# A first MLP on token tiles of 384, 384, 512, 512, 512 instead of six of 384, with single buffers for keys, queries and values

## The chip, the cores and the metric

The kernel runs on one core of one Trainium2 chip, as one program. The metric is the device time of an execution in microseconds (us). The kernel before takes 785.8 us, the median of three runs (784.78 to 785.98).

## The reference, cut to what matters

Three stages, all in fp32, over 4 batches x 576 positions = 2304 tokens of width 512 (8 heads x 64).

```
scores = q @ k.T / sqrt(64)                       # per batch and head, 576 x 576
masks  = plain window of 32 keys      (heads 0-3)
         32 keys at a stride of 4     (heads 4-7, "dilated")
x  = softmax(where(mask, scores, -1e9)) @ v       # laid out as tokens x 512
x  = max(x @ w1, x @ w2, x @ w3) @ w_out          # first MLP, 512 -> 768 -> 512
h  = x @ w_in                                     # second MLP, 512 -> 2048 -> 512
g  = (a0 + a1*h + a2*h^2 + a3*h^3) / (1 + |b0|*|h| + |b1|*h^2 + 1e-6)
out = g @ w_out
```

## The kernel before, in words

**Arithmetic.** Both MLPs keep the precision of fp32 with split operands: an operand is held as a high part (`x1h`, `hh`, `x2h`, `gh`) and a low part (`x1l`, `hl`, `x2l`, `gl`), and each product is three matmuls (`mm3`, L535 to L540): high x high, high x low, low x high. ScalarE (ACT) makes the high part with a copy, VectorE (DVE) the low part with a subtraction. The first MLP's weights come as 8-byte words and are converted on the chip in five steps named `L`, `up`, `bits`, `hi`, `lo`; the 32 tiles of the second MLP's weights are converted one per "tick" during the first MLP, put back to HBM as `w2d`, and fetched again as `w2s` by `load_w2` (L598), each fetch with a copy on ACT and a subtraction on DVE.

**Attention.** The tokens go through attention in 12 chunks of 192, three per batch. A chunk has a plain half (`p`) and a dilated half (`d`), and each runs `S` (scores on TensorE, PE), `MX` (mask add and row maximum, DVE), `D` (subtract, DVE), `E` (exp, ACT), `SM` and `SB` (sum and normalisation, DVE), `X` (transposes on PE in two groups) with `XC` (copies on ACT), `V` (times the values, PE), and `VH`, `VL` (the split of the result into `x1h` and `x1l`).

**First MLP.** It runs in six units of 384 tokens (`TU`). A unit has 18 groups of 12 matmuls (6 blocks of the inner width x 3 weight matrices; each group is followed by a copy or a maximum out of PSUM) and 4 groups of 18 for its output (`Y`), so 288 matmuls in 22 slots. The output goes to HBM as `x2d`.

**Second MLP.** Tiles of 512, 512, 512, 384, 384 tokens, 16 slices each: 12 matmuls make `h`, ACT and DVE evaluate the fraction, and 12 (or 9) matmuls add it into `acc`. A slice's `acc` matmuls stand three slices behind its `h` matmuls.

**Order of the work.** The table `START` writes out chunks 0 to 3 and unit 0 word by word; `W:n` puts 4n small matmuls on a zero tile in front (`keep_warm`, L177). From unit 1 on, unit u's groups are emitted one per slot, and beside each stands one row of the table `UNIT` for chunks 2(u+1) and 2(u+1)+1: two chunks during each of units 1 to 4, none during unit 5. Every engine runs its instructions in the order in which a scheduler then put them; the `order` rows below show that order. TensorE's weight loads run beside its matmuls.

**Buffers and queues.** Queries have two buffers per half (`QA`), keys two, values one; loads of the first chunks go on the SP queue, those of the later ones on POOL's, where the writes of `w2d` and `x2d` stand too. Of the 32 tiles of `w2s`, 7 (`W2A`) are fetched as the last unit starts, 18 as that unit gives up the first MLP's weights, and 7 after it (`w2c`, L746).

## Time and profile before

| | |
|---|---|
| median of 3 runs | 785.8 us |
| the profiled execution's own time | 785.84 us |
| its span, first to last instruction | 784.1 us |
| PE busy | 778.1 us, 99% |
| DVE busy | 589.5 us, 75% |
| ACT busy | 466.2 us, 59% |
| granted TensorE clock | 1.000 |

PE counts as busy while a matmul is in flight, and matmuls overlap, so a busy PE is read by the distance between the starts of neighbouring matmuls. "Idle before" names what ended an engine's wait. Times are us from the span's start, unless marked ns.

### The profile page before, as it was taken

The page shows a single profiled execution, that of the slowest core. Times are in us where ns is not written, and L with a number is a line of the kernel's source. Part 1 is how long each engine was busy: PE and PEld are TensorE (multiplying, and loading weights), DVE is VectorE, ACT ScalarE, POOL GpSimd, SP SyncE. Part 2 cuts the span into 40 slices and gives each one's busy share as a digit, 9 for nine tenths or more (in the row PEclk, how much of TensorE's full clock was granted, in tenths as well). Part 3 has the DMA queues.
Part 4 walks back from the last instruction along what each step waited for, and adds up shares of the span by engine and source line. Part 5 has one row for each costly group of instructions (what it writes and reads, how often), then busy time and mean ns, then how long its engine had stood idle before and what let it go on. Part 6 is the DMA issues. An engine that isn't in the chain of part 4 may idle for free.

```text
span 784.1 us, 12858 instructions
## 1 busy us (share of the span) xinstructions
PE 778.1 (99%) x4964; PEld 712.4 (91%) x4964; DVE 589.5 (75%) x1066; ACT 466.2 (59%) x907; POOL 55.8 (7%) x106
## 2 busy tenths in 40 slices
PE   9999999999999999999999999999999999999998
PEld 8999999999999999999988888888888889989996
DVE  5999366456465475367299999888988889888885
ACT  5898242332333333265397778766877678777774
POOL 0000221201211201100100001000010001000000
PEclk9999999999999999999999999999999999999999
DMA  9993346745655544184500011000110011000001
GB/s 335 405 407 122 127 154 217 247 134 189 214 173 189 174 144 161 44 292 123 173 0 1 1 54 54 1 1 0 41 55 0 1 41 54 1 1 22 21 0 41
DMA packets 28606, 86.52 MB, mean 110 GB/s; under 512 B 3664, under 2 KB 5328, under 8 KB 28544
## 3 DMA queue, kind: packets, MB, share of 16 engines
q1 hardware_dynamic: 20208, 55.41, 20.3%
q0 software_dynamic: 8336, 30.28, 11.0%
q8 instruction: 39, 0.64, 0.3%
q14 instruction: 23, 0.19, 0.1%
HBM read 67.85 MB, written 17.83 MB: 109 GB/s over the span
## 4 chain that ended last, share of the span: by engine, by line
PE 85%; issue 10%; DVE 2%; DMA 1%; POOL 1%; ACT 0%; POOLq 0%; SPq 0%; ACTq 0%; DVEq 0%
PE mm L538 9%; PE mm L539 9%; PE mm L540 9%; PE acc L826 8%; PE acc L825 8%; PE acc L827 8%; PE h L539 8%; PE h L540 8%; PE h L538 8%; PE sc L295 3%; PE tpp L374 2%; PE pv L405 1%; PE pv L397 1%; PE sc L179 1%; DMA raw<-in_w_in_dram 1%
## 5 line engine op out<-in xcount | busy, mean ns | idle before, releaser
L538 PE MATMUL mm<-x1h,w1s 128*128 128x384 f32 x432 | 146.8, 340 | 0.0
L539 PE MATMUL mm<-x1l,w1s 128*128 128x384 f32 x432 | 144.8, 335 | 0.0
L540 PE MATMUL mm<-x1h,w1s 128*128 128x384 f32 x432 | 144.5, 335 | 0.0
L540 PE MATMUL h<-x2h,w2s 128*128 128x512 f32 (+1 forms) x320 | 117.7, 368 | 0.0
L538 PE MATMUL h<-x2h,w2s 128*128 128x512 f32 (+1 forms) x320 | 117.6, 368 | 0.0
L539 PE MATMUL h<-x2l,w2s 128*128 128x512 f32 (+1 forms) x320 | 117.6, 367 | 0.0
L825 PE MATMUL acc<-w2s,gh 128*128 128x512 f32 x288 | 112.2, 389 | 0.2 <-ACT gh L806 0.2
L826 PE MATMUL acc<-w2s,gh 128*128 128x512 f32 x288 | 112.3, 390 | 0.0
L827 PE MATMUL acc<-w2s,gl 128*128 128x512 f32 x288 | 109.3, 390 | 0.0
L781 DVE SCALAR_TENSOR_TENSOR q<-q,cs,ab 128x512 f32<-128x512 f32 (+1 forms) x80 | 55.7, 696 | 37.8 <-ACT ab L775 37.5
L538 PEld LDWEIGHTS mm<-x1h,w1s 128*128 128x128 f32 x432 | 81.0, 188 | 1.0
L539 PEld LDWEIGHTS mm<-x1l,w1s 128*128 128x128 f32 x432 | 81.2, 188 | 0.0
L540 PEld LDWEIGHTS mm<-x1h,w1s 128*128 128x128 f32 x432 | 81.1, 188 | 0.0
L774 ACT ACTIVATE q<-h 128x512 f32<-128x512 f32 (+1 forms) x80 | 43.9, 548 | 58.8 <-PE h L540 57.8
L559 DVE TENSOR_TENSOR m<-mm,m 128x384 f32<-128x384 f32 x72 | 39.7, 553 | 40.4 <-PE mm L540 40.3
L539 PEld LDWEIGHTS h<-x2l,w2s 128*128 128x128 f32 x320 | 60.1, 188 | 8.1
L538 PEld LDWEIGHTS h<-x2h,w2s 128*128 128x128 f32 x320 | 60.0, 188 | 8.1
L540 PEld LDWEIGHTS h<-x2h,w2s 128*128 128x128 f32 x320 | 60.1, 188 | 7.5
L806 ACT ACTIVATE gh<-p 128x512 fp32r<-128x512 f32 (+1 forms) x80 | 47.6, 595 | 31.1 <-DVE p L800 30.4
L825 PEld LDWEIGHTS acc<-w2s,gh 128*128 128x128 f32 x288 | 54.1, 188 | 11.6 <-ACT gh L806 0.7
L827 PEld LDWEIGHTS acc<-w2s,gl 128*128 128x128 f32 x288 | 54.0, 188 | 11.3
L826 PEld LDWEIGHTS acc<-w2s,gh 128*128 128x128 f32 x288 | 54.0, 188 | 10.9
...
## 6 DMA issues: line engine op xcount, KB each, us to landing
...
```

The costliest lines, as they stand in the source:

```text
L295: nc.tensor.matmul(o[h], lhsT=lq[:, h], rhs=rk, start=not pem, stop=not pem or n % G == G - 1)
L374: nc.tensor.transpose(tp[:, i, :], sv[:, G * j + i, :], ident[:Q, :Q])
L538: nc.tensor.matmul(o, lhsT=lh, rhs=rh, start=(i == 0), stop=False)
L539: nc.tensor.matmul(o, lhsT=lh, rhs=rl, start=False, stop=False)
L540: pe_at[0] = nc.tensor.matmul(o, lhsT=ll, rhs=rh, start=False, stop=(i == n - 1))
L559: nc.vector.tensor_tensor(out=m1[u, f], in0=o, in1=m1[u, f], op=ALU.max)
L774: nc.scalar.activation(out=s["q"], in_=s["h"], func=AF.Square)
L781: nc.vector.scalar_tensor_tensor(out=s["q"], in0=s["q"], scalar=cs[:, 5:6], in1=s["ab"], op0=ALU.mult, op1=ALU.add)
L806: nc.scalar.activation(out=s["gh"], in_=s["p"], func=AF.Copy)
L825: nc.tensor.matmul(o, lhsT=gh, rhs=w[:, 0:512], start=(c == 0), stop=False)
L826: nc.tensor.matmul(o, lhsT=gh, rhs=w[:, 512:1024], start=False, stop=False)
L827: nc.tensor.matmul(o, lhsT=gl, rhs=w[:, 0:512], start=False, stop=(c == F2 - 1))
```

## The change

The first MLP's units become 384, 384, 512, 512, 512 tokens (`SZ1`), so that there are five: 288 matmuls each, the last three on 512 columns. A chunk of 192 can now end in the middle of a unit, so `pieces` writes its split into one or two units. The eight chunks after `START` go three during unit 1, three during unit 2, two during unit 3 (`FIRST`, `UNITS`), none during unit 4. The 36 ticks of the weight conversion are spread over 66 slots, not 88.

Buffers: queries and keys have one each (the next chunk's queries are fetched when this chunk's scores are done, the next batch's keys after the batch's last scores), batch 0's keys lie in an `x1` buffer and chunk 1's values where `hh` and `hl` come later, and `w2s` has 3 tiles at the last unit's start, 18 during it and 11 after it. The plain queries of chunks 0 to 3 come without the zero blocks of their block-diagonal form (`qf`, half the bytes); their scores are 12 matmuls of half the rows and columns, not 6. `START` is written anew.

```
-mk qp0 mkB kp0 W:14 S0:p qd0 MX0:p kd0 kp1 E0:p W:7 S0:d,mm qp1 SM0:p SB0:p,act MX0:d D0:d W:1 S1:p
...
+mkB mk qp0 kp0 W:8 S0:p,pv MX0:p qd0 kd0 E0:p W:7 S0:d,mm L SM0:p SB0:p qd1 W:5 X0:p,1,pv MX0:d D0:d
+up X0:p,0,pv XC0:p,0 kp1 qp1 W:1 S1:d E0:d bits hi SM0:d MX1:d S1:p,mm lo L XC0:p,1 E1:d v0 v1 qd2
...
-UNIT = """
...
+UNITS = {3: """
 Sa:p
...
-    TU = 2 * CH
-    NU = NT // TU
+    SZ1 = [384, 384, 512, 512, 512]
+    NU = len(SZ1)
+    AT1 = [sum(SZ1[:u]) for u in range(NU)]
+    T1 = max(SZ1)
+    FIRST = {2: 4, 3: 7, 4: 10}
...
-    W2A = 7
+    W2A = 3
...
-    spare = []
+    keys0 = {}
+
+    def unit_x1(u):
+        if u not in x1:
+            x1[u] = [com.tile([128, NP * T1], F32R, tag=tag, bufs=2, name=f"{tag}{u}")
+                     [:, 0:NP * SZ1[u]].rearrange("p (c t) -> p c t", c=NP)
+                     for tag in ("x1h", "x1l")]
+        return x1[u]
...
         if b not in at_k:
-            at_k[b] = (
-                at.tile([128, S // 32, 2, 32], F32, tag="kTp", bufs=2, name=f"kTp{b}"),
-                at.tile([128, 8, S // 4], F32, tag="kTd", bufs=2, name=f"kTd{b}"),
-            )
+            if b == 0:
+                for tag in ("x1h", "x1l"):
+                    keys0[tag] = com.tile([128, NP * T1], F32, tag=tag, bufs=2, name="keys0")
+                kTp, kTd = [keys0[tag][:, 0:2 * S] for tag in ("x1h", "x1l")]
+            else:
+                kTp, kTd = [at.tile([128, 2 * S], F32, tag=tag, name=f"{tag}{b}")
+                            for tag in ("kTp", "kTd")]
+            at_k[b] = (kTp.rearrange("p (n a t) -> p n a t", a=2, t=32),
+                       kTd.rearrange("p (n m) -> p n m", n=8))
         kTp, kTd = at_k[b]
-        queue = nc.sync if b < 3 else nc.gpsimd
+        queue = nc.sync if b < 2 else nc.gpsimd
...
-        queue = nc.sync if c < 3 * QA else nc.gpsimd
-        if g == "p":
-            t = at.tile([128, 2 * BP, 2 * QP], F32, tag="qTp", bufs=QA, name=f"qTp{c}")
-            queue.dma_start(out=t.rearrange("p n w -> p (n w)"), in_=qp_in[c])
-        else:
-            t = at.tile([128, 8, 2 * M], F32, tag="qTd", bufs=QA, name=f"qTd{c}")
-            queue.dma_start(out=t.rearrange("p n w -> p (n w)"), in_=qd_in[c])
+        queue = nc.sync if c <= MASK_PE else nc.gpsimd
+        pool = cv_p[0] if c in (1, 3) else at
+        src = qd_in[c] if g == "d" else qf_in[c] if c < MASK_PE else qp_in[c - MASK_PE]
+        n = src.shape[1]
+        t = pool.tile([128, n if pool is not at else 2 * BP * 2 * QP], F32, tag="qT" + g,
+                      name=f"qT{g}{c}")[:, 0:n]
+        queue.dma_start(out=t, in_=src)
+        t = t.rearrange("p (n w) -> p n w", n=8 if g == "d" else 2 * BP)
         at_raw[c, g] = t
...
+        if c == 1:
+            vp, vd = [com.tile([128, 2 * T1], F32, tag=f"hhl{f}", name=f"v1_{f}") for f in (0, 1)]
...
-                for h in (slice(0, QP), slice(QP, Q)) if plain and not pem else (slice(0, Q),):
-                    nc.tensor.matmul(o[h], lhsT=lq[:, h], rhs=rk,
+                for h in (slice(0, QP), slice(QP, Q)) if plain else (slice(0, Q),):
+                    if plain and pem:
+                        l, r = lq[h], rk[h]
+                    else:
+                        l, r = lq[:, h], rk
+                    nc.tensor.matmul(o[h], lhsT=l, rhs=r,
                                      start=not pem, stop=not pem or n % G == G - 1)
-            if c >= 2 * QA:
-                load_q(c + QA, g)
-            if g == "d" and ci == 0 and 1 < b < B - 1:
+            if c >= MASK_PE:
+                load_q(c + 1, g)
+            if g == "d" and ci == NC - 1 and 0 < b < B - 1:
                 load_k(b + 1)
...
-        def split_of(g):
-            pv = grp["v" + g]
+        def pieces(g):
             at_p = slice(0, 2) if g == "p" else slice(2, 4)
-            return pv, x1h[:, at_p, tok], x1l[:, at_p, tok]
+            t0, t1 = CH * c, CH * c + CH
+            for u in range(NU):
+                a, z = max(t0, AT1[u]), min(t1, AT1[u] + SZ1[u])
+                if a < z:
+                    h, l = unit_x1(u)
+                    to = slice(a - AT1[u], z - AT1[u])
+                    yield grp["v" + g][:, :, a - t0:z - t0], h[:, at_p, to], l[:, at_p, to]
 
         def VH(g):
-            src, dh, _ = split_of(g)
-            nc.scalar.activation(out=dh, in_=src, func=AF.Copy)
+            for src, dh, _ in pieces(g):
+                nc.scalar.activation(out=dh, in_=src, func=AF.Copy)
 
         def VL(g):
-            src, dh, dl = split_of(g)
-            nc.vector.tensor_sub(dl, src, dh.bitcast(F32))
+            for src, dh, dl in pieces(g):
+                nc.vector.tensor_sub(dl, src, dh.bitcast(F32))
...
-        for row in UNIT.strip().split("\n"):
+        first, some = FIRST[u], FIRST.get(u + 1, NCH) - FIRST[u]
+        for row in UNITS[some].strip().split("\n"):
             for word in row.replace("-", "").split():
                 op, _, arg = word.partition(":")
-                c = 2 * u + "abc".index(op[-1])
+                c = first + "abcd".index(op[-1])
...
-    def m1_mm(u, f, j, cols=slice(0, TU)):
+    def m1_mm(u, f, j, cols=None):
         if (u, f, j) not in m1:
-            m1[u, f, j] = bank("mm", "mm")[:, 0:TU]
+            m1[u, f, j] = bank("mm", "mm")[:, 0:SZ1[u]]
+        cols = cols or slice(0, SZ1[u])
...
-        hh = com.tile([128, TU], F32R, tag=f"hh{f}", name=f"hh{f}")
-        nc.scalar.activation(out=hh, in_=m1[u, f], func=AF.Copy)
-        m1["h", u, f] = [hh, None]
+        hhl = com.tile([128, 2 * T1], F32R, tag=f"hhl{f}", name=f"hhl{f}")
+        n = SZ1[u]
+        m1["h", u, f] = [hhl[:, 0:n], hhl[:, T1:T1 + n]]
+        nc.scalar.activation(out=hhl[:, 0:n], in_=m1[u, f], func=AF.Copy)
 
     def m1_hl(u, f):
-        hl = com.tile([128, TU], F32R, tag=f"hl{f}", name=f"hl{f}")
-        nc.vector.tensor_sub(hl, m1[u, f], m1["h", u, f][0].bitcast(F32))
-        m1["h", u, f][1] = hl
+        hh, hl = m1["h", u, f]
+        nc.vector.tensor_sub(hl, m1[u, f], hh.bitcast(F32))
...
-        for c in (4, 5):
-            for g in "pd":
-                load_q(c, g)
-        load_k(2)
+        for g in "pd":
+            load_q(4, g)
...
-                    if tick * TICK // 88 > (tick - 1) * TICK // 88:
+                    if tick * TICK // 66 > (tick - 1) * TICK // 66:
...
-    out["qp"] = qp_out.reshape(B * NC, 128, 2 * BP * 2 * QP)
+    qp_out = qp_out.reshape(B * NC, 2, D, 2 * BP, 2, QP)
+    first = np.stack([qp_out[0:4, j, :, :, j] for j in range(2)], 1)
+    out["qf"] = first.reshape(4, 128, 2 * BP * QP)
+    out["qp"] = qp_out[4:].reshape(B * NC - 4, 128, 2 * BP * 2 * QP)
```

**Where instructions moved.** First the SP queue at the very start, before and after. `mk` are the constants in two pieces, `qTp`, `qTd` the queries of the halves, `kTp`, `kTd` (later `keys0`) the keys, `w1r` raw weights.

```order
L639 DMA mk_138<-in_consts_dram 128x208
L217 DMA qTp0_142<-in_qp_dram 128x768
L640 DMA mk_138<-in_consts_dram 128x214
L206 DMA kTp0_145<-in_kp_dram 128x384
L220 DMA qTd0_220<-in_qd_dram 128x768
L209 DMA kTd0_146<-in_kd_dram 128x1152
```
```order
L687 DMA mk_138<-in_consts_dram 128x214
L686 DMA mk_138<-in_consts_dram 128x208
L258 DMA qTp0_143<-in_qf_dram 128x384
L244 DMA keys0_145<-in_kp_dram 128x384
L258 DMA qTd0_202<-in_qd_dram 128x768
L247 DMA keys0_146<-in_kd_dram 128x1152
```

Both pieces of the constants now stand first, and the first queries are half as wide.

Second DVE's queue in unit 1, from the dilated scores of chunk 5 to their normalisation. `sb` are the scores, `mx` and `sm` row maxima and sums, `m` the first MLP's maximum, `cvt` the weight conversion.

```order
L316 TENSOR_TENSOR sb_1879<-sc_1867,mk_138 96x320
L568 TENSOR_TENSOR hl5_1852<-m_1817,hh5_1850 128x384
L316 TENSOR_TENSOR sb_1879<-sc_1868,mk_138 96x320
L318 TENSOR_REDUCE mx_1880<-sb_1879 96x8
L332 TENSOR_TENSOR sb_1879<-sb_1879,mx_1880 96x640
L497 TENSOR_SCALAR cvt_1939<-cvt_1939 128x512
L499 SCALAR_TENSOR_TENSOR cvt_1939<-raw_1859,cvt_1939 128x512
L356 TENSOR_REDUCE sm_1881<-sb_1879 96x8
L360 TENSOR_SCALAR sm_1881<-sm_1881 96x8
L361 RECIPROCAL sm_1881<-sm_1881 96x8
L363 TENSOR_TENSOR sb_1879<-sb_1879,sm_1881 96x640
```
```order
L356 TENSOR_TENSOR sb_1716<-sc_1699,mk_138 96x320
L356 TENSOR_TENSOR sb_1716<-sc_1700,mk_138 96x320
L358 TENSOR_REDUCE mx_1717<-sb_1716 96x8
L372 TENSOR_TENSOR sb_1716<-sb_1716,mx_1717 96x640
L606 TENSOR_TENSOR m_1687<-mm_1731,m_1687 128x384
L543 TENSOR_SCALAR cvt_1746<-cvt_1746 128x512
L545 SCALAR_TENSOR_TENSOR cvt_1746<-raw_1694,cvt_1746 128x512
L396 TENSOR_REDUCE sm_1718<-sb_1716 96x8
L400 TENSOR_SCALAR sm_1718<-sm_1718 96x8
L606 TENSOR_TENSOR m_1687<-mm_1761,m_1687 128x384
L401 RECIPROCAL sm_1718<-sm_1718 96x8
L403 TENSOR_TENSOR sb_1716<-sb_1716,sm_1718 96x640
```

The chunk's half now falls between the groups of 12, and two maxima stand inside its chain; before, it fell into the output groups. On PE there are three groups of 12 matmuls between these scores and the transposes that need them, where chunk 4 before had four.

Third DVE's queue as the second MLP starts. `q`, `r`, `p` are the fraction's terms, `w2s` the last weight tiles, fetched after the first MLP.

```order
L606 TENSOR_TENSOR w2s25_4562<-w2s25_4562 128x512
L606 TENSOR_TENSOR w2s26_4566<-w2s26_4566 128x512
L781 SCALAR_TENSOR_TENSOR q_4625<-q_4625,cs_1376,ab_4626 128x512
L606 TENSOR_TENSOR w2s27_4570<-w2s27_4570 128x512
L606 TENSOR_TENSOR w2s28_4574<-w2s28_4574 128x512
L783 TENSOR_TENSOR p_4627<-h_4612,p_4627 128x512
L606 TENSOR_TENSOR w2s29_4578<-w2s29_4578 128x512
L606 TENSOR_TENSOR w2s30_4582<-w2s30_4582 128x512
L606 TENSOR_TENSOR w2s31_4586<-w2s31_4586 128x512
L784 SCALAR_TENSOR_TENSOR p_4627<-p_4627,mk_138,h_4612 128x512
L796 SCALAR_TENSOR_TENSOR q_4603<-q_4603,r_4631 128x512
```
```order
L653 TENSOR_TENSOR w2s24_4154<-w2s24_4154 128x512
L828 TENSOR_TENSOR p_4223<-h_4208,p_4223 128x512
L653 TENSOR_TENSOR w2s25_4158<-w2s25_4158 128x512
L653 TENSOR_TENSOR w2s26_4162<-w2s26_4162 128x512
L653 TENSOR_TENSOR w2s27_4166<-w2s27_4166 128x512
L829 SCALAR_TENSOR_TENSOR p_4223<-p_4223,mk_138,h_4208 128x512
L653 TENSOR_TENSOR w2s28_4170<-w2s28_4170 128x512
L653 TENSOR_TENSOR w2s29_4174<-w2s29_4174 128x512
L653 TENSOR_TENSOR w2s30_4178<-w2s30_4178 128x512
L653 TENSOR_TENSOR w2s31_4182<-w2s31_4182 128x512
L841 SCALAR_TENSOR_TENSOR q_4199<-q_4199,r_4227 128x512
```

Four more weight tiles (28 to 31) now stand directly ahead of slice 0's second step, the `q` from `q` and `r`. Tiles 21 to 23 stand above the second piece. PE's own order in this place is as before: six groups of `h`, then slice 0's `acc`.

## Rows read from the trace of the kernel before

**Rows 1.** The page, busy time, share and instructions of PE

```profile
PE 778.1 (99%) x4964; PEld 712.4 (91%) x4964; DVE 589.5 (75%) x1066; ACT 466.2 (59%) x907; POOL 55.8 (7%) x106
```

**Rows 2.** Waits of PE: waiting line, waited for, us in total, times, longest

```profile
PE pv L405 <- ACT pt L385: 0.5, 1, 0.5
```

**Rows 3.** Stages: length, then busy us of PE, PEld, DVE, ACT, POOL, clock, DMA

```profile
28.00:76.00 48.00, 48.00 (x393) 46.86 (x392) 46.83 (x101) 43.55 (x125) 0.00 (x0) 1.00 0.79 310
150.00:212.00 62.00, 62.00 (x522) 60.72 (x519) 36.00 (x73) 21.16 (x41) 11.64 (x22) 1.00 0.56 185
387.00:410.00 23.00, 22.77 (x100) 18.50 (x99) 20.05 (x32) 20.71 (x35) 0.00 (x0) 1.00 0.06 20
```

**Rows 4.** PE in order of time, unit 4's outputs, 384 columns: start, us

```profile
320.60 0.34 PE L539 MATMUL mm<-hl,wo1s 128*128 128x384 f32 x1
...
325.80 0.33 PE L539 MATMUL mm<-hl,wo1s 128*128 128x384 f32 x1
```

**Rows 5.** PE in order of time, second MLP, 512 columns

```profile
394.95 0.39 PE L538 MATMUL h<-x2h,w2s 128*128 128x512 f32 x1
...
401.30 0.39 PE L539 MATMUL h<-x2l,w2s 128*128 128x512 f32 x1
```

**Rows 6.** Groups by line and shape: count, busy us, mean ns

```profile
L538 PE MATMUL mm<-x1h,w1s 128*128 128x384 f32 x432 | 146.8, 340 | 0.0
```

**Rows 7.** PE in order of time around three transposes

```profile
326.15 0.49 PE L374 MATMUL tpp<-mk,sb 128*96 128x128 f32 x3
326.40 0.42 PE L538 MATMUL mm<-hh,wo1s 128*128 128x384 f32 x1
326.66 0.34 PE L539 MATMUL mm<-hl,wo1s 128*128 128x384 f32 x1
```

**Rows 8.** PE at the start, in order of time

```profile
0.99 5.47 PE L179 MATMUL sc<-warm 128*128 128x128 bf16 x56 [0.99 <-DVE warm L628]
6.30 0.41 PE L282 MATMUL sc<-mk 128*128 128x288 bf16 x2
...
27.59 0.42 PE L538 MATMUL mm<-x1h,w1s 128*128 128x384 f32 x1
```

**Rows 9.** DVE at the start, in order of time

```profile
4.47 0.17 DVE L682 TENSOR_SCALAR cs<-mk 128x4 f32<-128x4 f32 x1 [3.52 <-DMA mk<-in_consts_dram]
...
7.39 0.46 DVE L321 TENSOR_REDUCE mx<-sc 128x3 f32<-128x288 f32 x1 [2.49 <-PE sc L295]
...
26.16 1.02 DVE L421 TENSOR_TENSOR x1l<-pv,x1h 128x384 fp32r<-128x384 f32 x2
```

**Rows 10.** ACT as the second MLP starts, in order of time

```profile
394.82 1.67 ACT L605 ACTIVATE w2s<-w2s 128x512 fp32r<-128x512 f32 x3
396.39 0.72 ACT L791 ACTIVATE r<-r,cs 128x512 f32<-128x512 f32 x1
```

**Rows 11.** DVE in the same place

```profile
395.75 1.89 DVE L606 TENSOR_TENSOR w2s<-w2s 128x512 fp32r<-128x512 f32 x3
397.56 0.74 DVE L784 SCALAR_TENSOR_TENSOR p<-p,mk,h 128x512 f32<-128x512 f32 x1
398.22 0.68 DVE L796 SCALAR_TENSOR_TENSOR q<-q,r 128x512 f32<-128x512 f32 x1
```

**Rows 12.** PE in the same place

```profile
402.14 0.50 PE L825 MATMUL acc<-w2s,gh 128*128 128x512 f32 x1 [0.23 <-ACT gh L806]
```

**Rows 13.** Groups by line and shape, the dilated half's chain and the maximum

```profile
L559 DVE TENSOR_TENSOR m<-mm,m 128x384 f32<-128x384 f32 x72 | 39.7, 553 | 40.4 <-PE mm L540 40.3
...
L316 DVE TENSOR_TENSOR sb<-sc,mk 96x320 f32<-96x320 f32 x12 | 5.8, 482 | 0.3
L363 DVE TENSOR_TENSOR sb<-sb,sm 96x640 f32<-96x640 f32 x7 | 5.7, 821 | 0.2
...
L345 ACT ACTIVATE sb<-sb 96x640 f32<-96x640 f32 x6 | 4.4, 733 | 2.2 <-DVE sb L332 2.1
```

**Rows 14.** DMA issues: engine, count, KB each, us from issue to landing

```profile
qTp<-in_qp_dram POOLq DMA_DIRECT2D x6, 384.0 KB, 5.5
```

More of the change, by code (lines that the diff above doesn't have):

```diff
@@ L56 @@
+M:17 hi HH:5 HL:2 VH3:p lo lo lo HL:5 VH2:d V3:d VH3:d Y:3 VL2:p VL2:d Y:0 YS:3 Y:1 YS:1 Y:2 YS:0
+YS:2 VL3:d VL3:p
+"""
+UNITS = {3: """
+Sa:p
+MXa:p Ea:p
+SBa:p Sa:d MXa:d Ea:d Xa:p,1
+Xa:p,0 SBa:d
+-
+Xa:d,1 Xa:d,0
+Va:p Va:d Sb:p
+VEa:d VEa:p
+MXb:p Eb:p
+SBb:p Sb:d MXb:d Eb:d Xb:p,1
+Xb:p,0 SBb:d
+-
+Xb:d,1 Xb:d,0
+Vb:p Vb:d Sc:p
+VEb:d VEb:p
+MXc:p Ec:p
+SBc:p Sc:d MXc:d Ec:d Xc:p,1
+Xc:p,0 SBc:d
+-
+Xc:d,1 Xc:d,0
+Vc:p Vc:d Sd:p
+VEc:d VEc:p
+""", 2: """
 Sa:p
+-
 -
@@ L64 @@
 Va:p Va:d Sb:p
-VEa:d
--
-VEa:p
--
--
-MXb:p
--
-Eb:p SBb:p Sb:d MXb:d Xb:p,1
-Eb:d
-Xb:p,0
-SBb:d Xb:d,0
-Xb:d,1 Vb:p Vb:d Sc:p VEb:d VEb:p
-"""
+VEa:d VEa:p
+-
+-
+MXb:p Eb:p
+SBb:p Sb:d MXb:d Eb:d Xb:p,1
+Xb:p,0 SBb:d
+-
+-
+Xb:d,1 Xb:d,0
+Vb:p Vb:d Sc:p
+VEb:d VEb:p
+-
+"""}
 @with_exitstack
@@ L233, in load_v @@
         queue = nc.sync if c < 4 else nc.gpsimd
-        pool = cv_p[0] if c in (1, 3) else at
-        vp = pool.tile([128, BP, NP, D], F32, tag="vp", name=f"vp{c}")
-        queue.dma_start(out=vp.rearrange("p i h d -> p (i h d)"), in_=vp_in[c])
-        vd = pool.tile([128, NP, 4 * D], F32, tag="vd", name=f"vd{c}")
-        queue.dma_start(out=vd.rearrange("p h e -> p (h e)"), in_=vd_in[c])
+        if c == 1:
+            vp, vd = [com.tile([128, 2 * T1], F32, tag=f"hhl{f}", name=f"v1_{f}") for f in (0, 1)]
+        else:
+            vp = at.tile([128, BP * NP * D], F32, tag="vp", name=f"vp{c}")
+            vd = at.tile([128, NP * 4 * D], F32, tag="vd", name=f"vd{c}")
+        vp, vd = vp[:, 0:BP * NP * D], vd[:, 0:NP * 4 * D]
+        queue.dma_start(out=vp, in_=vp_in[c])
+        queue.dma_start(out=vd, in_=vd_in[c])
+        vp = vp.rearrange("p (i h d) -> p i h d", i=BP, h=NP)
+        vd = vd.rearrange("p (h e) -> p h e", h=NP)
         at_raw[c, "v"] = (vp, vd)
@@ L242, in attn_pieces @@
         b, ci = divmod(c, NC)
-        u, part = divmod(c, 2)
-        tok = slice(CH * part, CH * part + CH)
         kTp, kTd = at_k[b]
-        if c == 0:
-            spare.append(com.tile([128, NP * TU], F32, tag="x1h", bufs=2, name="spare"))
-        if part == 0:
-            x1[u] = (com.tile([128, NP, TU], F32R, tag="x1h", bufs=2, name=f"x1h{u}"),
-                     com.tile([128, NP, TU], F32R, tag="x1l", bufs=2, name=f"x1l{u}"))
-        x1h, x1l = x1[u]
         m0, nmk = dil(ci)
@@ L293, in SC @@
                     o = o.rearrange("q (n t) -> q n t", t=32)
-                for h in (slice(0, QP), slice(QP, Q)) if plain and not pem else (slice(0, Q),):
-                    nc.tensor.matmul(o[h], lhsT=lq[:, h], rhs=rk,
+                for h in (slice(0, QP), slice(QP, Q)) if plain else (slice(0, Q),):
+                    if plain and pem:
+                        l, r = lq[h], rk[h]
+                    else:
+                        l, r = lq[:, h], rk
+                    nc.tensor.matmul(o[h], lhsT=l, rhs=r,
                                      start=not pem, stop=not pem or n % G == G - 1)
-            if c >= 2 * QA:
-                load_q(c + QA, g)
-            if g == "d" and ci == 0 and 1 < b < B - 1:
+            if c >= MASK_PE:
+                load_q(c + 1, g)
+            if g == "d" and ci == NC - 1 and 0 < b < B - 1:
                 load_k(b + 1)
             if c == 1:
-                at0 = 0 if plain else 2 * BP * WP
                 ww = WP if plain else WD
-                sb = spare[0][:Q, at0:at0 + U * ww].rearrange("p (u w) -> p u w", w=ww)
+                sb = keys0["x1l" if plain else "x1h"][:Q, 2 * S:2 * S + U * ww]
+                sb = sb.rearrange("p (u w) -> p u w", w=ww)
             else:
@@ L590, in m1_ys @@
     def m1_ys(u, c):
-        xs = com.tile([128, TU], F32, tag="m", bufs=MB, name="xs")
+        xs = com.tile([128, T1], F32, tag="m", bufs=MB, name="xs")[:, 0:SZ1[u]]
         nc.scalar.activation(out=xs, in_=m1[u, "y", c], func=AF.Copy)
-        nc.gpsimd.dma_start(out=x2d[:, c, TU * u:TU * u + TU], in_=xs)
+        nc.gpsimd.dma_start(out=x2d[:, c, AT1[u]:AT1[u] + SZ1[u]], in_=xs)
     n2 = [0]
@@ L669 @@
                     f, j = divmod(int(arg), 3)
-                    m1_mm(0, f, j, slice(CH if (0, f, j) in m1 else 0, TU))
+                    m1_mm(0, f, j, slice(CH if (0, f, j) in m1 else 0, 2 * CH))
                 elif op == "M":
```

37 lines of the change are left out of this document (17 added, 20 removed).

## The prediction

> **What bounds the kernel now.** I read the page first, then PE's waits, then the busy time stage by stage, then PE in order of time. PE is busy 778.1 of 784.1 us [rows 1], and after its first instruction the longest wait that the view of PE's waits names is one of 0.5 us [rows 2]. A busy PE alone proves little, since its matmuls overlap, so the reader is to look at the distance between starts. In unit 4's outputs 30 matmuls of 384 columns go from 320.60 to 325.80 [rows 4], 0.1733 us each; in the second MLP 28 of 512 columns go from 394.95 to 401.30 [rows 5], 0.2268 us each (I use 0.2267). Neither run has a hole. So from the first matmul of unit 0 at 27.59 [rows 8] PE is the bound, and the time is the sum of what PE issues, plus whatever makes it wait. DVE has room in a middle unit (36.0 of 62 us), none in unit 0 (46.83 of 48) and little as the second MLP starts (20.05 of 23) [rows 3]. Those two places are where the change can make PE wait.
>
> **Fewer matmuls.** The rows give 0.2267 - 0.1733 = 0.0534 us for 128 columns, 0.160 us for 384, so each matmul costs 0.0133 us beyond its columns. Units of 288 matmuls (the 432 of one line and kind [rows 6] are six units' 72) go from six to five, on the same number of columns: before 1728 x 0.1733 = 299.5 us, now 576 x 0.1733 + 864 x 0.2267 = 295.7 us. Exact pitches of 0.17333 and 0.22667 give -3.84 us. All of it lies on the path, because PE is the path. The first MLP's matmuls have run at 512 columns in no row; those of the second MLP have the same 128 x 128 weights and pitch at 384, so I take their 512. Bounds: -3.84, and 0 if the pitch went with the columns.
>
> [...]
>
> **More restarts.** Three transposes start at 326.15 and the next matmul at 326.40, but the one behind it comes 0.26 us later, not 0.173 [rows 7]: each return to the MLP costs 0.087 us. By the order of PE's instructions the first MLP is interrupted 44 times before and 50 times now: 6 x 0.087 = +0.5 us. The plain scores of chunk 3, in 12 halves now, lie behind the first matmul as well; no row shows such halves there, and I bound them by their six extra instructions at the same 0.087, 0.5 us either way, and take 0.
>
> **The start.** PE's first 56 small matmuls run from 0.99 to 6.30, 0.095 us each [rows 8]; now there are 32, which end at 4.1. Then chunk 0 needs its constants, plain queries and first keys. The second piece of the constants was third in SP's queue, behind 107 + 384 KB, and landed at 4.47 [rows 9] when 595 KB were through; now 107 + 104 + 192 + 192 = 595 KB are everything that chunk 0's plain scores need. So they start at about 4.6, not 6.5. Chunk 0's normalisation goes from ACT to DVE, one more pass of 128x576. I followed the three queues forward with each row's own duration: the first row maximum at 5.7 (before 7.39 [rows 9]), chunk 1's plain transposes at about 21.2, the last split `x1l` at 25.5 to 26.0 (before it ends at 27.2, 26.16 + 1.02 [rows 9]), the first MLP matmul at 26.0, not 27.59: -1.6 us. Against that, by then one conversion less is through DVE than before, and unit 0 has DVE 98% full [rows 3], so some of the gain comes back as waits of PE for weights, or for the last `hl` before the outputs. I take 0.4 back: -1.2 us. Bounds: 0 (DVE ends unit 0 no earlier than before) and -2.4 (the 24 small matmuls, 24 x 0.095, with nothing late).
>
> **Three chunks in a unit.** Of chunk 5's dilated half in unit 1, DVE and ACT must do, between the scores and the transposes, two adds (0.48 each), a maximum, a subtraction, a sum and a product (0.82 each, taken as the product), an exp (0.73) and now two of the MLP's maxima (0.55 each) [rows 13], with a conversion under the exp: 0.96 + 3.28 + 0.73 + 1.1 + some 0.4 of what shows of the conversion = 6.5 us. PE has three groups of 12 x 0.1733 and two bursts of 0.34 [rows 4, 7] in the meantime, 6.9 us; chunk 4's half had four groups before, 9.0 us. In units 2 and 3 groups are 2.72 us, which restores the slack. I take +0.2 us for chunks 4 and 5; bounds 0 and the slower rival below.
>
> Single buffers: the next chunk's queries leave once this chunk's scores are done and land 5.5 us later [rows 14], keys likewise, and need not be there for some seven slots of over 2 us. POOL's queue has only two weight writes between them and the scores. Cost 0. [...] Here the row's 5.5 us against seven slots is the overlap without a second buffer; were each of the eight chunks to wait for its load, it would be 8 x 5.5 = 44 us.
>
> **The start of the second MLP.** Eleven weight tiles come late, not seven, and four more stand on DVE directly ahead of slice 0's second step, which was at 398.22 [rows 11]. ACT needs 0.56 us for each (1.67 for three [rows 10]) and has them, with one other instruction, behind the exp that ends at 397.1 [rows 10]; DVE needs 0.60 each in a row (three from 395.75 to 397.56 [rows 11]). So DVE's second step goes from 398.22 to 398.22 + 4 x 0.60 = 400.6, and ACT's `gh` with it, for which PE waits 0.23 us already at 402.14 [rows 12]. PE has nothing else in its queue: the six groups of `h` ahead of it are the same, and the fourth PSUM buffer comes free as before. The four passes are thus paid in full: +2.4 us. Bounds: 0 (the tiles finish early and a wait elsewhere falls away) and +3.5 (ACT's four copies and its `Square` of slice 2 come on top in part). Behind that nothing changes: with PE later by the same amount DVE stands no worse than before.
>
> **Nothing.** The conversion's 36 ticks now fill three units, not four; DVE had 26 of 62 us free there. The last unit's 18 tiles have 65 us, not 50.
>
> **Sum.** -3.84 + 0.5 - 1.2 + 0.2 + 2.4 = -1.9 us. From the profiled execution's own 785.84 us (span 784.1; it lies within 0.1 us of the median 785.8) that is **783.9 us**.
>
> **Rivals.**
> (a) The last weight tiles cost nothing and no chain is late: 783.9 - 2.6 = 781.3 us. For it: only their place in the queue speaks for a wait. Against: PE waited for just this `gh` before.
> (b) The start gives nothing, because DVE sets unit 0's end: 783.9 + 1.2 = 785.1 us. For it: 98% busy. Against: it also starts 1.7 us earlier.
> (c) Slower: with three chunks in a unit the attention chains end after PE's cover, and PE waits at the transposes of both halves. The point from which this decides is a chain longer than 6.9 us in unit 1, or 9.0 in units 2 and 3; at 0.5 us for each of 8 x 2 halves it is 8 us, 791.9 us. For it: my 6.5 is near 6.9. Against: only chunks 4 and 5 are near.
> (d) The pitch goes with the columns, 0.2311 at 512: the 3.84 us are gone, 787.8 us. The second MLP's rows speak against it. [...]
> (e) Loads of the single buffers show: 828 us. The 5.5 us speak against it.
>
> **Numbers.** My case 0.55 (its own range 782.4 to 785.4), (a) 0.18, (b) 0.12, (c) 0.10, (d) 0.03, (e) 0.02. About 0.2%, 1.6 us, is what a measurement of this kernel can tell from no change, so faster means below 784.2. That is all of (a), 0.65 of my case and a little of (b): 0.55. Same takes the rest of my case, most of (b) and half of (d): 0.31. Slower: (c), (e) and the rest of (d): 0.14. The range from 780.6 to 787.5 takes in (a) with 0.7 us of extra gain at the start, (b), and the upper bound of the second MLP's start; it leaves out (c), (e) and most of (d).
>
> **What would show it.** Starts 0.2267 us apart in units 2 to 4 (the main term). The first MLP matmul near 26.0, and unit 0's outputs 1 to 2 us earlier. A PE wait for `gh` of 2 to 3 us about 16 us into the second MLP. No wait of PE at a transpose above 0.5 us. I am wrong if PE waits for weights in unit 0 by more than 1 us, if transposes wait in units 2 or 3, or if the `gh` wait stays at 0.2.

## The result and the profile after

The changed kernel takes **794.1 us** (median of six runs, 790.88 to 795.07) against 785.45 for the kernel before beside it: ratio 1.0103, 95% interval 1.0083 to 1.0122. It is slower; 783.9 was predicted. Its profiled execution took 792.2 us, with a span of 790.4.

The page's line of busy time, to hold against [rows 1]:

```profile
PE 775.4 (98%) x4696; PEld 671.2 (85%) x4696; DVE 589.6 (75%) x1053; ACT 461.0 (58%) x889; POOL 56.2 (7%) x107
```

PE issues 268 matmuls fewer than before, and the span is 6.3 us longer, so PE stands still somewhere or runs more slowly. The view of PE's waits (waiting line, waited for, us in total, times, longest), where [rows 2] had nothing above 0.5:

```profile
PE acc L870 <- ACT gh L851: 2.6, 1, 2.6
PE tpp L414 <- ACT pt L425: 2.6, 2, 1.3
PE tpp L414 <- ACT cvt L537: 2.2, 1, 2.2
...
PE sc L335 <- DMA keys<-in_kd_dram: 0.8, 1, 0.8
```

Four waits above 0.5 us stand behind the first MLP matmul: two at chunk 5's transposes in unit 1 (1.29 us at the plain half's, 2.20 at the dilated half's), one in unit 2 (1.33), one in the second MLP. By stage (stretch, its length, then busy us of PE, PEld, DVE, ACT, POOL, granted clock, DMA share, GB/s), to hold against [rows 3]:

```profile
100.00:160.00 60.00, 56.04 (x529) 52.87 (x528) 37.49 (x79) 20.95 (x44) 14.43 (x27) 0.97 0.65 216
160.00:240.00 80.00, 78.53 (x535) 65.34 (x534) 49.32 (x93) 26.94 (x49) 15.03 (x28) 1.00 0.61 201
400.00:420.00 20.00, 17.36 (x77) 14.03 (x76) 20.00 (x34) 18.79 (x32) 0.00 (x0) 1.00 0.00 0
```

In 100 to 160 the granted clock is 0.97 as well. PE alone, in that place (PE busy, clock, DMA share, GB/s):

```profile
126.00:127.00 1.00, 0.00 (x0) 1.00 1.02 419
127.00:128.00 1.00, 0.78 (x6) 0.79 0.96 369
128.00:131.00 3.00, 3.00 (x13) 0.50 0.67 264
131.00:132.00 1.00, 1.00 (x14) 1.00 0.00 0
```

Behind the second wait the granted clock is 0.50 from 128 to 131. From 127.50 to 131.10 PE issued nine MLP matmuls and a burst of transposes; at 0.1733 us each and 0.34 for the burst [rows 4, 7] these take 1.9 us, so this cost about 1.7 us more.

The stages by PE's first matmul in each, in the two profiled executions:

| | before | after | difference |
|---|---|---|---|
| first MLP matmul | 27.59 | 26.61 | -0.98 |
| unit 0 | 60.14 | 60.80 | +0.66 |
| eight later chunks' attention, with waits | 47.94 | 55.88 | +7.94 |
| matmuls of the other units | 249.72 | 245.76 | -3.96 |
| second MLP, first `h` to last `acc` | 394.41 | 396.78 | +2.37 |
| last matmul's start | 779.80 | 785.83 | +6.03 |

(The third row is the length of the units behind unit 0 less 49.92 us for one of 384 tokens and 65.28 for one of 512; -3.96 is -3.84 and the 0.12 by which the last unit before was longer than its matmuls.)

The table cuts by MLP units, and a little work of attention crossed a cut. Half of chunk 4's plain scores now runs in unit 0 (in the kernel before, chunk 4's scores begin in unit 1, at 91.99):

```profile
76.92 0.72 PE L335 MATMUL sc<-kTp,qTp 128*64 128x96 f32 x12
77.57 0.44 PE L585 MATMUL mm<-hhl,wo1s 128*128 128x384 f32 x1
```

The MLP matmuls around it start 0.91 and 0.28 us apart, not 0.173, so it takes some 0.87 us with its restart. Counted with the other chunks' attention, unit 0 is 0.2 us shorter than before, and the eight chunks take 8.8 us more, not 7.9.

**What happened in unit 1.** Chunk 5's dilated scores end at 116.6 (115.08 and 1.51). ACT, DVE and PE around that moment, each in order of time:

```profile
118.85 0.66 ACT L537 ACTIVATE cvt<-raw 128x512 f32<-128x512 f32 x1 [3.96 <-DMA raw<-in_w_in_dram]
...
119.78 0.48 ACT L425 ACTIVATE pt<-tpp 96x384 f32<-96x384 f32 x1
```

```profile
119.54 0.43 DVE L543 TENSOR_SCALAR cvt<-cvt 128x512 int32<-128x512 int32 x1 [3.64 <-ACT cvt L537]
...
120.61 0.88 DVE L356 TENSOR_TENSOR sb<-sc,mk 96x320 f32<-96x320 f32 x2
...
126.25 0.82 DVE L403 TENSOR_TENSOR sb<-sb,sm 96x640 f32<-96x640 f32 x1
```

```profile
115.08 1.51 PE L335 MATMUL sc<-kTd,qTd 128*96 128x80 f32 x16
116.42 0.49 PE L414 MATMUL tpp<-mk,sb 128*96 128x128 f32 x3
...
120.31 0.53 PE L414 MATMUL tpp<-mk,sb 128*96 128x128 f32 x3 [1.29 <-ACT pt L425]
...
127.22 0.51 PE L414 MATMUL tpp<-mk,sb 96*80 96x96 f32 x4 [2.20 <-ACT cvt L537]
```

ACT stands at a conversion whose weight tile has not landed. Behind it in its queue is the copy (`pt`) that frees the buffer for the second group of the plain half's transposes (96 rows of 128): PE's first wait. DVE's part of that conversion waits for ACT, and behind it stands the mask add of the dilated scores, which were ready at 116.6. It starts at 120.61, and the normalisation ends at 127.07: PE's second wait, at the dilated half's transposes (80 rows of 96). (The view names ACT's `cvt` there, which ended at 127.22; what the transposes need is DVE's product.) My theory was that the weight tile's lateness and the conversion's place in the queues make the chain late; its rivals, that three chunks in a unit leave too little cover whatever the conversion does, or that its work is too much.

### The profile page after: what moved, and what is told of

It is laid out like the page before. It is cut to its first block, busy times and chain, and to the rows that moved or that the text cites. A ratio compares the mean times of both kernels' runs of the same rounds, so it can differ in the third digit from the quotient of the medians.

```text
span 790.4 us, 12266 instructions
## 1 busy us (share of the span) xinstructions
PE 775.4 (98%) x4696; PEld 671.2 (85%) x4696; DVE 589.6 (75%) x1053; ACT 461.0 (58%) x889; POOL 56.2 (7%) x107
## 4 chain that ended last, share of the span: by engine, by line
PE 91%; DMA 3%; DVE 3%; ACT 1%; issue 1%; SPq 0%; DVEq 0%; ACTq 0%
PE mm L584 12%; PE mm L585 12%; PE mm L586 11%; PE acc L872 8%; PE acc L871 8%; PE acc L870 8%; PE h L586 8%; PE h L584 8%; PE h L585 8%; PE sc L335 3%; DMA raw<-in_w_in_dram 2%; PE tpp L414 2%; PE pv L445 2%; PE pv L437 1%; DMA keys<-in_kd_dram 1%
## 5 line engine op out<-in xcount | busy, mean ns | idle before, releaser
L584 PE MATMUL mm<-x1h,w1s 128*128 128x512 f32 (+1 forms) x360 | 136.0, 378 | 0.0
L585 PE MATMUL mm<-x1l,w1s 128*128 128x512 f32 (+1 forms) x360 | 133.3, 370 | 0.0
L586 PE MATMUL mm<-x1h,w1s 128*128 128x512 f32 (+1 forms) x360 | 133.0, 369 | 0.0
L584 PEld LDWEIGHTS mm<-x1h,w1s 128*128 128x128 f32 x360 | 68.0, 189 | 8.8
L586 PEld LDWEIGHTS mm<-x1h,w1s 128*128 128x128 f32 x360 | 68.0, 189 | 8.5
L585 PEld LDWEIGHTS mm<-x1l,w1s 128*128 128x128 f32 x360 | 68.1, 189 | 7.9
L851 ACT ACTIVATE gh<-p 128x512 fp32r<-128x512 f32 (+1 forms) x80 | 47.5, 593 | 31.1 <-DVE p L845 30.3
L821 ACT ACTIVATE p<-h,cs 128x512 f32<-128x512 f32 (+1 forms) x80 | 59.0, 737 | 0.0
```

The source lines that it names most:

```text
L584: nc.tensor.matmul(o, lhsT=lh, rhs=rh, start=(i == 0), stop=False)
L585: nc.tensor.matmul(o, lhsT=lh, rhs=rl, start=False, stop=False)
L586: pe_at[0] = nc.tensor.matmul(o, lhsT=ll, rhs=rh, start=False, stop=(i == n - 1))
L821: nc.scalar.activation(out=s["p"], in_=s["h"], func=AF.Identity, scale=cs[:, 3:4], bias=cs[:, 2:3])
L851: nc.scalar.activation(out=s["gh"], in_=s["p"], func=AF.Copy)
```

## The experiments

**1. The late tiles one per slice.**

```
-        while n2[0] < len(order2):
-            load_w2(w2c)
...
             if g < NSL:
                 dve_a(g)
+            if 1 <= g and n2[0] < len(order2):
+                load_w2(w2c)
```

> The eleven late weight tiles of the second MLP are prepared one per slice from slice 1 on, not all ahead of slice 0's second step. Theory: PE's wait of 2.64 us for gh at 408.17 comes only from their place on DVE's queue; it falls to 0.3 us or less, nothing later waits, and the median goes from 794.1 to 791.6 us (-2.5). Rival: DVE is 94% busy between 420 and 500, so the tiles' 11 x 0.6 us come back as waits of PE for gh or gl in slices 2 to 12; total unchanged within 1 us, 793 to 795.

Measured: 791.2 us (790.41 to 792.05), ratio to before 1.0070 (1.0055 to 1.0085). PE never waits for `gh` or `gl`; from the first `h` to the last `acc` it takes 393.95 us, not 396.78. The theory holds, the rival is out. The profile showed something else: the first MLP matmul came at 28.68, and the clock had fallen behind the wait for the first dilated keys (PE order; then windows of PE):

```profile
9.29 1.53 PE L335 MATMUL sc<-keys,qTd 128*96 128x48 f32 x16 [1.30 <-DMA keys<-in_kd_dram]
10.66 2.20 PE L205 MATMUL tpp<-warm 128*128 128x128 bf16 x20
```

```profile
9.00:10.00 1.00, 0.71 (x9) 1.00 1.02 405
11.00:14.00 3.00, 3.00 (x25) 0.50 1.04 409
```

The 20 small matmuls take 1.28 us in the changed kernel's own profile, where the wait was 0.79 us.

**2. No conversion in unit 1.**

```
-                if not last:
+                if not last and u > 1:
                     tick += 1
-                    if tick * TICK // 66 > (tick - 1) * TICK // 66:
+                    if tick * TICK // 44 > (tick - 1) * TICK // 44:
```

> The conversion of the second MLP's weights starts with unit 2 and runs in 44 slots, none of it in unit 1. Theory (a conversion's load lands late, ACT stands at cvt, DVE behind it, and the attention chain with them): PE's waits at the transposes of unit 1 (1.29 and 2.20 us) fall below 0.5 us in sum, unit 1 goes from 75.2 to about 70 us, the granted clock stays 1.00 between 100 and 160; unit 2 has one tick per 1.2 slots and may wait 1 to 3 us more than its 1.5. Median 788 to 790. Rival (with three chunks in a unit the attention chain alone outlasts PE's cover): the transposes of unit 1 still wait for 2 us or more, median within 1.5 us of 794.1.

Measured: 794.3 us (791.39 to 796.79), ratio 1.0115 (1.0081 to 1.0149). Unit 1 takes 68.7 us, not 75.2, without a wait: three chunks fit, and the rival on the chain alone is out. But unit 2 takes 90.1, not 85.2, with waits that sum to 3.7 us and a clock of 0.96 in 160 to 245. The waits are 2.4 us more than the 1.3 of the changed kernel's profile, within the 1 to 3 more that I had allowed; the fall of the clock I had not counted. Moving the conversion moved the loss. PE in unit 2:

```profile
202.97 0.50 PE L414 MATMUL tpp<-mk,sb 96*80 96x96 f32 x4 [1.23 <-DVE sb L403]
206.90 0.86 PE L414 MATMUL tpp<-mk,sb 96*80 96x96 f32 x4 [2.48 <-ACT pt L425]
```

**3. A longer lead for the load, first try.** In `cv_tick` a tile is converted two ticks behind its load:

```
+            if upto > n_w1:
+                if name == "up" and due < upto:
+                    due -= 1
+                elif name == "bits":
+                    due = cv_at["up"]
```

> The same conversion ticks in the same slots, but a weight tile is converted two ticks after its load was issued, not one, with DVE's part in the same tick. Theory (it is the lateness of the load, not the conversion's work): ACT's waits at cvt for the raw tile fall from 59.7 us to under 25, PE's waits at transposes in units 1 and 2 (4.8 us) to under 1.5, the clock stays at 1.00, median 787 to 789. Rival (the work of the conversion on DVE and ACT, 1.1 and 0.66 us a tick, is what the chain has no room for): waits at transposes stay above 3 us, median 792 to 795.

Measured: 793.1 us (790.52 to 794.41), ratio 1.0090 (1.0069 to 1.0111), the same waits at the same places, ACT idle 60.8 us ahead of the conversion. This decides nothing: the scheduler put the conversion where it stood before, and the order on ACT, DVE and PE is the same as in the changed kernel. Experiment 6 repeats it properly.

**4. Experiments 1 and 2 together.**

> Late tiles one per slice and the conversion from unit 2 on, together. Theory: the two gains add, -2.5 and -4 to -6 us: median 785.5 to 787.5, and the spread of the runs shrinks from 4 us to below 1.5 because no wait lets the clock fall. Rival: either gain fails as told of the two kernels apart; median 789 or more.

Measured: 790.0 us (785.79 to 793.49), ratio 1.0053 (1.0037 to 1.0069): the gain of the late tiles, and the unit 2 of experiment 2 (91.0 us). The rival's side. The ten runs go with their mean clocks, from 785.79 us at 0.999 to 793.49 at 0.992.

**5. 20 more warm matmuls in front of the dilated scores.** `W:7 S0:d` becomes `W:12 S0:d`.

> 20 more of the small keep-warm matmuls (48, not 28) stand on PE between chunk 0's plain and dilated scores, where PE waits 0.5 to 1.3 us for the dilated keys; nothing else changes. In two of the profiles so far (the kernel with the late tiles, and that with the conversion from unit 2 on) the granted clock was at half level from about 10.7 to 14 us and the first MLP matmul came at 28.7, not 26.6. Theory (the wait for the keys behind the shorter warm-up decides whether the clock falls, in some runs and not in others): the first MLP matmul is at 26.5 to 27.1 in the profile with the clock at 1.00 up to 26, and the median is 1 to 2 us below 794.1, at 792 to 793, with a highest run of 794 or less. Rival (the late unit 1 alone makes the spread, the start only shifts): the median stays at 793.5 to 795 with the same spread.

Measured: 793.0 us (791.85 to 793.55), ratio 1.0097 (1.0083 to 1.0110). The wait for the dilated keys is gone and the spread is smaller, but in the profile the first MLP matmul was at 29.15. PE had waited 0.72 us for the first plain keys and then ran more slowly. PE's rows there, in the changed kernel and in this one:

```profile
5.03 1.21 PE L335 MATMUL sc<-keys,qTp 64*64 64x96 f32 x24
6.17 1.74 PE L205 MATMUL sc<-warm 128*128 128x128 bf16 x28
```

```profile
5.79 2.18 PE L335 MATMUL sc<-keys,qTp 64*64 64x96 f32 x24 [0.72 <-DMA keys<-in_kp_dram]
7.91 3.53 PE L205 MATMUL sc<-warm 128*128 128x128 bf16 x48
```

This is not a fall. In both profiles the first 32 small matmuls start 0.107 us apart, and later ones 0.056: PE begins at about half its later rate. In the changed kernel the 24 plain-score matmuls already run at the higher one (1.21 us); here they take 2.18, and the higher rate comes only from about 9.4, by the starts of the 48. The views' granted clock reads 1.00 from 0 to 15 in both, so it does not show this. The theory had only one of the two waits. Unit 1 takes 72.6 us in this profile, not 75.2, with the clock at 1.00 behind a wait of 2.21 us, so the gain of the median need not all come from the start.

**6. The conversion held until its tile is there.** Experiment 3, and a wait of ACT's step for a PE matmul:

```
-        nc.scalar.activation(out=t, in_=cv[i][1].bitcast(F32), func=AF.Prelu, scale=SHRINK,
-                             alpha=-(2.0 ** 32))
+        up = nc.scalar.activation(out=t, in_=cv[i][1].bitcast(F32), func=AF.Prelu, scale=SHRINK,
+                                  alpha=-(2.0 ** 32))
+        if conv_seq[i][0] == "w2":
+            tc.add_manual_dep(up.ins, pe_at[0].ins.name, PACE, reason="the load first")
```

> A weight tile's conversion on ACT also waits for the PE matmul that stands two ticks behind its load, so in ACT's queue it comes about five instructions later, behind the copies of the transposes; same number of ticks, same slots. (The kernel before this, with the two ticks but without the wait, left ACT's order as it was.) Theory (the conversion stands in front of attention's work before its load has landed): ACT's idle time ahead of cvt for raw tiles falls from 59.7 us to under 25, PE's waits at transposes in units 1 and 2 from 4.8 to under 1.5 us, unit 1 from 75.2 to 69 to 70 us, the clock between 100 and 160 is 1.00, and the median is 788 to 790. Rival (with the conversion's work in it the chain is too long in whatever order): waits at transposes above 3 us, unit 1 above 73 us, median 792 to 795.

Measured: **785.0 us** (784.26 to 786.32), ratio 1.0001 (0.9992 to 1.0010): 9 us less than the changed kernel by the medians, more than I expected. Units 1 and 2 take 68.8 and 83.2 us, not 75.2 and 85.2, PE is busy without a gap from 100 to 240, and the clock is 1.00 there. Number of ticks and work are the same. What ACT stood idle for ahead of the conversion (us, times), in the kernel before, the changed one and this one:

```profile
  DMA raw<-in_w_out_dram: 23.7, 14
  DMA raw<-in_w_in_dram: 22.4, 15
```

```profile
  DMA raw<-in_w_in_dram: 37.2, 15
  DMA raw<-in_w_out_dram: 22.5, 11
```

```profile
  PE mm L594: 33.2, 13
```

ACT still waits, but for a PE matmul that comes when the order says, and no longer for a DMA. The edit changes two things, the load's lead and the conversion's place in the queues; since experiment 3 left the order as it was, no run has one without the other. Chunk 5's dilated half now, on DVE and on PE:

```profile
116.06 0.49 DVE L356 TENSOR_TENSOR sb<-sc,mk 96x320 f32<-96x320 f32 x1 [0.27 <-PE sc L335]
...
122.61 0.82 DVE L403 TENSOR_TENSOR sb<-sb,sm 96x640 f32<-96x640 f32 x1
```

```profile
115.20 1.51 PE L335 MATMUL sc<-kTd,qTd 128*96 128x80 f32 x16
...
118.98 0.49 PE L414 MATMUL tpp<-mk,sb 128*96 128x128 f32 x3
123.58 0.50 PE L414 MATMUL tpp<-mk,sb 96*80 96x96 f32 x4
```

The chain takes 116.06 to 123.43, 7.4 us with two tiles' conversions in it. It begins with the first half of the scores, 0.65 us before the last of them ends (115.20 and 1.51), so it is done when PE comes for it at 123.58, 6.9 us after the scores. The runs lie in two groups, 784.3 to 785.0 (six) and 785.6 to 786.3 (five, all at a mean clock of 0.997, the others at 0.999 or more). The profile, one of the second group, shows what differs: here the clock fell behind the 2.64 us wait for `gh` (0.57 in 400 to 404), and from that matmul to the last it takes 379.23 us, not the 377.66 of the changed kernel's profile, whose clock held behind the same wait (1.00 in 400 to 420).

```profile
399.00:400.00 1.00, 0.00 (x0) 1.00 0.00 0
400.00:404.00 4.00, 3.94 (x10) 0.57 0.00 0
```

**7. Experiments 1, 5 and 6 together.**

> The held conversion, the late tiles one per slice and the 20 more warm matmuls together. Theory: the losses are separate and all three go: first MLP matmul near 27, units 1 to 3 about 69.5, 84 and 76 us, no gh wait, clock 1.00 throughout: 783 to 785.5, not slower than the kernel before. Rival: one of them comes back at another place; 787 or more.

Measured: **781.8 us** (781.56 to 783.92), ratio 0.9961 (0.9949 to 0.9974), faster than the kernel before. No wait of PE behind 19 us. The profiled execution was the run of 783.92. As in experiment 5 PE still runs at the lower rate behind the wait for the plain keys, here of 0.65 us: the 24 plain-score matmuls take 2.18 us, not 1.21, and the first MLP matmul is at 29.29.

**8. The keys' loads 5 us later.**

```
+                if b >= 2:
+                    tc.add_manual_dep(ld.ins, pe_at[0].ins.name, PACE, reason="keys later")
```

> Changed kernel with one change: the plain keys of batches 2 and 3 (576 KB in two transfers), which with one buffer leave right behind the plain scores of a batch's last chunk (109.65, beside values, queries and the weight tile), also wait for the MLP matmul ahead of that chunk's dilated scores, 5 us later. Theory (the single buffers put these loads onto the weight tile's, which then takes 7.4 us to land, not 4.1): the tile that ACT waits for until 118.85 lands 1 to 2 us earlier and PE's 1.29 us at 120.31 falls by that, to 0.3 or less; the 2.20 at 127.22 falls in part, to 0.5 to 1.5; unit 1 71 to 73.5 us, median 789 to 792. Rival (the transfers matter nothing, only the place of the conversion in ACT's queue): both waits as before within 0.5 us, unit 1 above 74.5.

Measured: 796.5 us (796.10 to 799.99), ratio 1.0149 (1.0123 to 1.0175). In the changed kernel values, queries and 576 KB of keys leave on POOL's queue from 107.18 on, and the weight tile that leaves at 111.16 is not there until 118.85, 7.7 us later. POOL's queue there:

```profile
107.18 0.55 POOL L279 DMA_DIRECT2D vp<-in_vp_dram  x1 [2.41 <-PE pv L437]
...
109.65 1.08 POOL L244 DMA_DIRECT2D kTp<-in_kp_dram  x2
```

And ACT, then PE, with the keys later:

```profile
115.97 0.67 ACT L539 ACTIVATE cvt<-raw 128x512 f32<-128x512 f32 x1 [1.65 <-DMA raw<-in_w_in_dram]
...
126.13 0.66 ACT L539 ACTIVATE cvt<-raw 128x512 f32<-128x512 f32 x1 [2.30 <-DMA raw<-in_w_in_dram]
```

```profile
124.39 0.50 PE L416 MATMUL tpp<-mk,sb 96*80 96x96 f32 x4 [1.39 <-DVE sb L405]
127.60 0.72 PE L416 MATMUL tpp<-mk,sb 96*80 96x96 f32 x4 [1.96 <-ACT pt L427]
```

The tile that left at 110.64 is converted at 115.97, and the wait of 1.29 us is gone: these loads did delay it. But the delayed loads meet the tile of 118.58, and PE waits 1.39 + 1.96 us at the dilated half's transposes. Unit 1 is 74.8 us. The theory is right that these loads delay the tile, and wrong on the gain; unit 2, which I had not thought of, is 2.9 us longer, and the profile's mean clock is 0.993, not 0.997. That the single buffers bring the loads together was part of the theory, and this experiment doesn't test it (see below).

**9. Experiment 7 with 48 warm matmuls at the very start**, not 32 (`W:12 S0:p`).

> As the kernel with all three, with 48 warm matmuls, not 32, ahead of chunk 0's plain scores as well. Theory: in the profile of that kernel the clock fell there, behind a wait of 0.65 us for the first keys (first MLP matmul at 29.3); with the wait filled it never falls, the first MLP matmul is at 26.9 to 27.5, all runs lie within 1 us of each other and the median is 781 to 782.2. Rival: the longer warm-up delays chunk 0 by its full 0.9 us and the clock had fallen in one run of five only: 782.3 to 783.

Measured: 782.1 us (781.67 to 783.02), ratio 0.9954 (0.9940 to 0.9968). What the expectation calls a fall is the full rate that comes late in experiment 7. With 48 the plain scores run at the higher rate (1.21 us for the 24), and no run's mean clock is below 0.999, but PE waits 0.74 us for the dilated keys, which come at 10.48 here, and the first MLP matmul is at 28.23. The median is no better than experiment 7's, and the runs lie 1.35 us apart, not 1; between theory and rival.

**10. The kernel before with 32 warm matmuls, not 56** (`W:8` for `W:14`).

> Kernel before with one change: 32 warm matmuls ahead of the first scores, not 56. Theory (the shorter warm-up leaves PE waiting for the first keys and the second piece of the constants, and that lets the clock fall): PE waits 1 to 2 us at the first masks or scores, in some runs the granted clock is at half level for 2 to 4 us behind it, and the median goes from 785.4 to 786 to 787.5 with a spread above 1.5 us. Rival (chunk 0's first scores are set by the transfers, and the clock needs nothing there): first MLP matmul at 27.6 as before, median within 0.5 us of 785.4.

Measured: 786.2 us (785.08 to 788.08), ratio 1.0008 (0.9997 to 1.0020): the median cannot be told from before, and since the kernel before had a run of 788.56 beside it, the spread proves nothing either. Three of the ten runs have a mean clock of 0.997 or 0.998 (786.3, 787.5, 787.7). The profile is one of them and shows the theory's course (PE waits, the clock is at 0.68 in 7 to 10, the 28 small matmuls take 3.00 us, not 1.73, and the first MLP matmul comes at 28.72):

```profile
6.49 1.55 PE L295 MATMUL sc<-kTp,qTp 128*128 128x96 f32 x12 [1.55 <-DMA kTp<-in_kp_dram]
7.88 3.00 PE L179 MATMUL sc<-warm 128*128 128x128 bf16 x28
```

**11. Experiments 1 and 6, the start as changed.**

> The held conversion and the late tiles one per slice, with the start of the changed kernel as it is (32 and 28 warm matmuls). Theory (the two waits on PE behind unit 0 are separate losses, and the start is a third that falls in some runs only): unit 1 at 69 us, the second MLP 2.8 us shorter than in the changed kernel, no wait of PE above 0.5 us behind 26 us; runs in two groups, near 781.3 where the clock holds at the start and near 783.4 where it falls, median 781 to 783.5. Rival (the 20 more warm matmuls gave part of the 781.8 of all three together): median 783.5 or more, all runs above 782.5.

Measured: **781.9 us** (781.36 to 783.75), ratio 0.9961 (0.9948 to 0.9975). Unit 1 is 69.5 us, with a last wait of 0.65 at a transpose; four runs lie at 781.4 to 782.1 and two at 783.7 (mean clock 0.998). So the two edits behind unit 0 give all of it, and the longer warm-ups nothing that the median shows. This is the simplest version that beats both kernels: 12.2 us less than the changed one, 3.8 less than before.

## Why the prediction was wrong

**Failed: "Three chunks in a unit".** The term was +0.2 us, with +0.5 for restarts; together they came out at +8.8 (the table's 7.9 and the 0.87 in unit 0), 8.1 more than forecast, and that is the whole 8 us by which the profile missed the sum. Of the 8.8, 4.8 are the three waits, 1.7 the clock and some 0.5 the restarts; the other 1.8 I can't assign in full (shorter waits of 0.31 and 0.16 us at unit 1's outputs are in it). The sum of the chain was not far off: 7.4 us in experiment 6, against 6.5 predicted; its two conversions alone hold DVE for 2.2 us (0.43 + 0.68 + 0.41 + 0.68). What failed is "some 0.4 of what shows of the conversion". I priced it as work that fills gaps, when on both engines it is a wait in a queue: ACT stood 3.96 us for a tile, the mask add of ready scores came 4.0 us late, and PE's transposes waited. The plain half's transposes had no term at all. "Nothing" fails with it: I measured the denser ticks against DVE's free time, not against what stands behind them. The trace of before had the sign: ACT stood idle 46.1 us ahead of these conversions for tiles that had not landed. That cost PE nothing while two chunks shared a unit; with three, the chain and the transposes' copies are behind it. Experiments 2 and 6 show it from two sides.

**Not settled: "Single buffers ... Cost 0".** No PE wait behind the start names keys, queries or values, as I said: each load is early enough for itself. I had not asked what a load delays, and in experiment 8 a weight tile is converted 5.3 us after its issue, not 7.7, once the keys leave later. But that the single buffers bring these loads together is not shown. In the kernel before, with two buffers for queries and keys, the same transfers leave as closely behind chunk 5's plain scores (POOL's queue, then SP's):

```profile
115.81 0.55 POOL L236 DMA_DIRECT2D vp<-in_vp_dram  x1
...
117.43 1.09 POOL L206 DMA_DIRECT2D kTp<-in_kp_dram  x2
```

```profile
123.28 0.33 SPq L478 DMA_DIRECT2D raw<-in_w_out_dram  x1
```

There the next weight tile leaves 5.3 us behind the last of the keys (117.97 and 123.28), and no tile takes more than 5.0 us to land; in the changed kernel one leaves 1.0 us behind them (110.18 and 111.16). No run has the second buffers.

**Missed: the clock.** No step counted it, because it is 1.00 throughout in the profile of before (one of that kernel's later runs, 788.56 us, has a mean of 0.997). Here it falls behind waits from 1.30 us (experiment 1, at the start) to 2.64 (experiment 6, in the second MLP), in some executions and not in others: about 1.7 us in unit 1, 1.6 at the start (28.68 against 26.61, of which 0.43 are the later keys), 1.6 in the second MLP (379.23 against 377.66). The same 2.64 us did it in one profile (experiment 6, 0.57 in 400 to 404) and not in another (the changed kernel, 1.00 in 400 to 420). The median lies 1.9 us above the profiled run, and the runs go with their mean clocks: 0.999 at 790.88 us, 0.997 at 792.2 (the profiled one, with its one fall), 0.995 or 0.996 in the four from 793.84 to 795.07. That those four have a second fall, and where, is argued, not shown: they left no trace.

**The start, -1.2:** -1.2 by the end of unit 0 where the clock holds (first matmul -0.98, unit 0 -0.2 without the shifted scores), and a loss where it falls (first matmul at 28.68 in experiment 1) or the full rate comes late (29.15 in experiment 5). The sum is partly luck: I had -1.6 for the first matmul and +0.4 for unit 0. The 0.095 us of a small matmul was a mean of two rates, 0.107 and 0.056, so the 32 ended at about 4.4, not 4.1. (The second piece of the constants stood behind 104 + 384 KB, not 107 + 384; the 595 are right.) I bounded the term by 0, "DVE ends unit 0 no earlier"; that cutting the warm-up could cost time was not among the bounds.

**Right.** The matmuls: unit 4's 288 go from 323.77 to 389.05, 0.2267 us each, so -3.84 holds and rival (d) is out. The start of the second MLP: +2.4 predicted, +2.37 measured, with PE waiting for `gh` 16.5 us in.

```profile
323.77 0.39 PE L584 MATMUL mm<-x1h,w1s 128*128 128x512 f32 x1
...
389.05 0.39 PE L584 MATMUL h<-x2h,w2s 128*128 128x512 f32 x1
...
408.17 0.50 PE L870 MATMUL acc<-w2s,gh 128*128 128x512 f32 x1 [2.64 <-ACT gh L851]
```

More restarts, +0.5: with the waits gone, the eight chunks of experiment 6 take 47.5 us beside the matmuls, and 0.87 for the scores in unit 0 (there at 77.16) make it 48.4; before, 47.9.

**The rivals.** (c) gave 791.9, near the 792.2 of the profile, and its deciding point was passed, a chain longer than 6.9 us (116.6 to 127.07 is 10.5). But it is not what happened: three transposes wait, not sixteen, for 4.8 us, not 8, and the cause is not the three chunks alone. (a) had 781.3, and experiment 11 comes to 781.9 once both causes of waiting are gone.
